# Attention's TensorE stream tied to program order, x written a unit later, no pairs of v beside the last rows' scores

## The chip, the cores and the metric

The kernel runs on one NeuronCore of a Trainium2 chip. The metric is device time in microseconds, the median of three runs: 1057.58 us before the change (1056.65 to 1059.66). Engines are named as in the profile: PE is TensorE, DVE is VectorE, ACT is ScalarE, POOL is GpSimd, SP is SyncE.

## The reference, cut to what matters

Attention over 4 batches, 8 heads, 576 positions and 64 dimensions, with a learned bias on the distance of two positions; then a mixture of eight experts that picks one for each token; then a dense block. All in 32-bit floats.

```python
scores = scale * q @ k^T + bias          # [4, 8, 576, 576]
attn   = exp(scores - max);  attn /= sum(attn) + 1e-9
x      = attn @ v                        # -> [2304, 512]
logits = x @ w_gate + modality_bias[modality_id];  e = argmax(logits)
x      = gate * (relu(x @ w1[e]) @ w2[e])
h      = x @ w_in;  out = (h * sigmoid(1.702 * h)) @ w_out
```

## The kernel before

Three stages follow each other: attention (to about 360 us of the span), routing and experts, the dense block. Only attention's code is touched.

Attention works in 16 groups g = 4 * hp + b (a pair of heads hp of one batch b). A group has five units: c = 0 to 3 are 128 rows of queries of both heads, c = 4 is the last 64 rows of both heads together. The list `order` holds all 80 units. Groups 0 to 3 are interleaved at first; from unit 20 on (group 4) a group's five units stand in a row, so that unit 5g + c is row block c of group g. The loop over i (L732 ff.) works at unit u = i + 2 on several things:

- `qkT(u)`, the scores: for c < 4 twelve matmuls into two buffers of PSUM (sc, one for each head, each half the array's rows, written in turn so that the two heads' matmuls run beside each other), for c = 4 six matmuls into one. DVE adds the bias and takes the maximum (L570, p, one instruction for each head), ACT takes the exponential (L574) and sums each row into rs.
- `tps(i)`, two units later: the exponentials p are transposed on PE through PSUM (tp_0, tp_1: four transposes each, tp_r: one) and copied into pt. DVE copies tp_0, ACT copies tp_1 and tp_r (L597, L599, L602). For c = 4 there are tp_0 and tp_r alone, and of each ACT copies one head (L608, L612) and DVE then the other (L609, L613); the DVE copy waits for the ACT copy.
- the product with v, in pieces from the list `todo`: `rest` (L639, one matmul that opens the sum in PSUM, pv) and four `pair`s (L645, two and two in two units). A group has two such products: part 0 for c = 0 and 1 (256 columns), part 1 for c = 2, 3 and 4 (320 columns). After the last pair ACT copies pv into xt (L649).
- `xs()`, called x below: xt is turned and multiplied with the gate's weights on PE (L666, L669, six matmul passes for part 1 and four for part 0), and DVE makes the logits and the output rows from it (Lp L685, xo L701 and L707), which go to X in DRAM.
- two steps of the next group's q and k: ACT rounds them (qh L524), DVE takes the rest (ql L529).
- now and then a step that prepares a block of the dense weights (cva, wh, wl: L168 to L195), and in the last groups sums of the logits (Lacc L692).

PSUM has three pools here: psb with two buffers for the scores, pst with three for tp and x, psv with a single one for pv. A buffer is written again only when its reader is done: pv's first matmul of a product waits for the copy xt of the product before, and an x that follows tp_0, tp_1 and tp_r takes the buffer of tp_0 and so waits for DVE's copy of it.

The order on each engine is not the code's order. A scheduler goes through the code, weighs costs and places each instruction when it thinks its inputs ready; `tc.keep_in_program_order` or `issue_after` bind single ones. The engines then take their instructions strictly in the order that came out. Once built, tp, p, sc and so on carry the unit's number, pv, xt and x the group's and the part's: sc51_0 are the scores of head 0 in unit 51 (c = 1 of group 10), x9_0 is x of part 0 of group 9.

Of the kernel before, what the change touches and what calls it, by code (L numbers as in the profile page):

```python
# [9 lines left out]
F32 = mybir.dt.float32  # L10
# [105 lines left out]
def body(ctx, tc, qk, vv, few, mid, ew1, ew2, ww, cst, alog, out, dbg=None):  # L116
    nc = tc.nc
    pe, act, dve, pool, sp = nc.tensor, nc.scalar, nc.vector, nc.gpsimd, nc.sync
# [10 lines left out]
    psv = acx.enter_context(tc.tile_pool(name="psv", bufs=1, space=PSUM))  # L129

    pso = None

    def big(name):
        return psb.tile([128, 2, 512], F32, tag="big", name=name)
# [143 lines left out]
    def routing_prepare(rp):  # L278
        def tl(name, *shape, dt=F32):
            V[name] = rp.tile([128, *shape], dt, name="r_" + name)  # L280
            return V[name]
        V["tl"] = tl
        pool.tensor_copy(tl("tri", 128, dt=F16), cc(C_TRI, 128))
        pool.memset(tl("ones", 128, dt=F16), 1.0)
        pool.tensor_copy(tl("iota", 128, dt=F16), cc(C_IOTA, 128))
        pool.memset(tl("zz", E * NTILE), 0.0)
        pool.memset(tl("cum", 1 + E * NTILE), 0.0)
        pool.memset(sn, 1)
        tl("mx", NTILE), tl("m2", NTILE), tl("dl", NTILE, E), tl("sc", NTILE, E), tl("A", E, NTILE, dt=F16)
# [162 lines left out]
    def attention():  # L452
        cx = ExitStack()
        kp = cx.enter_context(tc.tile_pool(name="akeep", bufs=1))
        p2 = cx.enter_context(tc.tile_pool(name="a2", bufs=2))
# [63 lines left out]
        def prep_steps(g):  # L519

            def hi(h):
                if h == 0:
                    hi_[g] = own(g, "qh", [128, 2, 640], F32R)
                act.copy(hi_[g][:, h], raw[g][:, h])  # L524

            def lo(h):
                if h == 0:
                    lo_[g] = own(g, "ql", [128, 2, 640], F32R)
                dve.tensor_tensor(lo_[g][:, h], raw[g][:, h], hi_[g].bitcast(F32)[:, h], op=ALU.subtract)  # L529
            return [lambda: hi(0), lambda: hi(1), lambda: lo(0), lambda: lo(1)]  # L530

        un = {}
        grp = {}
        todo = []


        order = [(0, 0), (1, 0), (0, 1), (1, 1), (2, 0), (2, 1), (3, 0), (3, 1)]
# [41 lines left out]
        def tps(i):  # L579
            g, c = order[i]  # L580
            G = grp[g]
            p = un.pop(i)["p"]
            half = 0 if c < 2 else 1
            if c in (0, 2):
                w_ = 256 if c == 0 else 320
                G["pt", half] = p2.tile([128, 9, 320], F32, tag="pt", name=f"pt{g}_{half}")[:, :, :w_]
            pt = G["pt", half]
            if c < 4:
                col = 128 * (c - 2 * half)
                for h in range(2):  # L590
                    ps = pst.tile([128, 512], F32, tag="t", name=f"tp{i}_{h}")
                    for cc in range(4):
                        c0 = 640 * h + 128 * cc
                        pe.transpose(ps[:, 128 * cc:128 * cc + 128], p[:, c0:c0 + 128], ident)  # L594
                    dst, src = pt[:, 4 * h:4 * h + 4, col:col + 128], ps.rearrange("p (c r) -> p c r", c=4)
                    if h == 0:
                        dve.tensor_copy(dst, src)  # L597
                    else:
                        act.copy(dst, src)  # L599
                ps = pst.tile([128, 512], F32, tag="t", name=f"tp{i}_r")  # L600
                pe.transpose(ps[:, :128], p[:, 512:640], ident)
                act.copy(pt[:, 8, col:col + 128], ps[:, :128])  # L602
            else:
                ps = pst.tile([128, 512], F32, tag="t", name=f"tp{i}_0")
                for cc in range(4):
                    pe.transpose(ps[:, 128 * cc:128 * cc + 128], p[:, 128 * cc:128 * cc + 128], ident)
                s_ = ps.rearrange("p (c h r) -> p h c r", c=4, h=2)
                act.copy(pt[:, 0:4, 256:320], s_[:, 0])  # L608
                dve.tensor_copy(pt[:, 4:8, 256:320], s_[:, 1])  # L609
                ps = pst.tile([128, 512], F32, tag="t", name=f"tp{i}_r")  # L610
                pe.transpose(ps[:64, :128], p[:, 512:S], ident)
                act.copy(pt[0:64, 8, 256:320], ps[0:64, 0:64])  # L612
                dve.tensor_copy(pt[64:128, 8, 256:320], ps[0:64, 64:128])  # L613
            if c == 1:
                todo.extend(pv_pieces(g, 0))
            if c == 3 and g == 15:
                *pv, G["xs"] = pv_pieces(g, 2)
                todo.extend(pv)
            if c == 4:
                if g == 15:  # L620
                    *pv, xs = pv_pieces(g, 3)
                    todo.extend(pv + [G["xs"], xs])
                else:
                    todo.extend(pv_pieces(g, 1))

        def pv_pieces(g, part):


            G = grp[g]
            hp, b = divmod(g, B)  # L630
            half = min(part, 1)
# [10 lines left out]
            def pair(cc):  # L642
                ps = G["ps", part]
                for h in range(2):
                    pe.matmul(ps[64 * h:64 * h + 64, :W], lhsT=vm[g][:, 256 * h + 64 * cc:256 * h + 64 * cc + 64],  # L645
                              rhs=G["pt", half][:, 4 * h + cc, cols], start=False, stop=cc == 3)
                if cc == 3:
                    xt = G["xt", part] = p2.tile([128, 320], F32, tag="xt", name=f"xt{g}_{part}")[:, :W]
                    act.copy(xt, ps[:, :W])  # L649
                    ri = G["ri", part] = p2.tile([128, 3, 2], F32, tag=f"ri{half}", name=f"ri{g}_{part}")  # L650
                    if main:
                        dve.tensor_scalar_add(ri[:, 0:2], G["rs", 2 * half], 1e-9)
                    if tail:
                        pool.memset(ri[64:128, 2, :], 1.0)
                        for h in range(2):
                            dve.tensor_scalar_add(ri[0:64, 2, h:h + 1], G["rs", 4][64 * h:64 * h + 64], 1e-9)
                    used = ri[:, 0 if main else 2:3 if tail else 2]
                    dve.reciprocal(used, used)
# [63 lines left out]
            def two(a):  # L722
                for cc in (a, a + 1):
                    pair(cc)
            return [(rest, lambda: two(0)), (None, lambda: two(2)), (xs, None)]

        load_qkv(1)
        nT = 0
# [3 lines left out]
        vcx = ExitStack()  # L732
        NU = 80
        pend = []
        for i in range(-2, NU + 6):
            u = i + 2
            if u < NU:
                while nT < need.get(u, 36):
                    bias_step(nT)
                    if nT in (1, 4):  # L740
                        for f in prep_steps(0 if nT == 1 else 1):
                            f()
                    if nT % 8 == 0 and nT:
                        load_bias(0, nT // 8 - 1)
                    nT += 1
                    if nT == 36:
                        bias_evac()
                        load_bias(0, 4)
                        bcx.close()
                        modality()  # L750
                if u == 25:
                    ecx.close()
                    wpool["w0"] = ctx.enter_context(tc.tile_pool(name="w0", bufs=1, side="right"))
                    routing_prepare(rcx.enter_context(tc.tile_pool(name="rp", bufs=1, side="right")))
                    wpool["cv"] = vcx.enter_context(tc.tile_pool(name="cv", bufs=1, side="right"))
                    early = conv_list(list(range(4)))
                if u in starts:
                    load_qkv(starts[u])
                    pend = prep_steps(starts[u])


            if u >= NU and i < NU:
                tps(i)
            steps = todo[:1]
            if len(todo) > 1 and (not todo[0][1] or len(todo) > 4 and todo[1][1]):
                steps = todo[:2]
            del todo[:len(steps)]
            if 0 <= i and u < NU:
                tps(i)
            for whole, _ in steps:  # L770
                if whole:
                    whole()
            if u < NU:
                qkT(u)
            for _, half in steps:
                if half:
                    half()
            for _ in range(3 if u < 8 else 2):
                if pend and (u < 8 or u not in starts):
                    pend.pop(0)()  # L780
            if early and u % 2:
                early.pop(0)()
        assert not todo
        while early:
            early.pop(0)()
        vcx.close()
# [338 lines left out]
```

## Time and profile before

| | |
|---|---|
| median of three runs | 1057.58 us |
| the profiled execution, its own time | 1058.45 us |
| its span | 1056.8 us |
| PE busy over the span | 1012.0 us (96%) |
| DVE, ACT busy over the span | 749.5 us (71%), 629.9 us (60%) |
| attention's steady part, unit 24 to unit 79 | 143.77 to 347.12 us, 203.35 us, eleven cycles |

The profile lists busy time by engine, the waits (who waited for whom), and timelines with each group of instructions in order of time. Matmuls are pipelined: the duration of a row is longer than its distance to the next, so the cost of a block on PE is read from the start of its row to the start of the next block's row. The steady part repeats every five units, from the scores of c = 4 of one group to those of the next; this is called a cycle below.

### The profile page before, as it was taken

The page shows a single profiled execution, that of the slowest core. Times are in us where ns is not written, and L with a number is a line of the kernel's source. Part 1 is how long each engine was busy: PE and PEld are TensorE (multiplying, and loading weights), DVE is VectorE, ACT ScalarE, POOL GpSimd, SP SyncE. Part 2 cuts the span into 40 slices and gives each one's busy share as a digit, 9 for nine tenths or more (in the row PEclk, how much of TensorE's full clock was granted, in tenths as well). Part 3 has the DMA queues.
Part 4 walks back from the last instruction along what each step waited for, and adds up shares of the span by engine and source line. Part 5 has one row for each costly group of instructions (what it writes and reads, how often), then busy time and mean ns, then how long its engine had stood idle before and what let it go on. Part 6 is the DMA issues. An engine that isn't in the chain of part 4 may idle for free. (4 is left out here: it accounts for less than half of the span.)

```text
span 1056.8 us, 17322 instructions
## 1 busy us (share of the span) xinstructions
PE 1012.0 (96%) x6030; PEld 810.5 (77%) x6030; DVE 749.5 (71%) x1476; ACT 629.9 (60%) x1203; POOL 131.1 (12%) x136
## 2 busy tenths in 40 slices
PE   6899999999999679999999999999999999999997
PEld 2447666676676458888888888999998899999996
DVE  7977777787877789999999984734574566464433
ACT  7867667676666469999899973534432333232221
POOL 6400000000000153651111000000000000001212
PEclk9999999999999889999999999999999999999999
DMA  8755412523410151511252352400220112010111
GB/s 285 259 174 171 123 45 85 184 82 93 143 43 18 53 184 38 203 41 51 80 187 83 101 178 94 139 31 21 61 80 1 41 44 77 1 40 31 48 43 60
DMA packets 46939, 98.08 MB, mean 93 GB/s; under 512 B 7424, under 2 KB 16896, under 8 KB 46848
## 3 DMA queue, kind: packets, MB, share of 16 engines
q1 hardware_dynamic: 41904, 80.90, 24.0%
q0 software_dynamic: 4800, 15.73, 4.2%
q8 instruction: 49, 0.80, 0.3%
q14 instruction: 42, 0.34, 0.1%
q10 hardware_dynamic: 144, 0.29, 0.1%
HBM read 146.57 MB, written 25.84 MB: 163 GB/s over the span
## 5 line engine op out<-in xcount | busy, mean ns | idle before, releaser
L828 DVE TENSOR_TENSOR wl<-wraw,wh 128x1024 fp32r<-128x1024 f32 x167 | 198.3, 1241 | 7.1 <-ACT wh L826 4.9
L826 ACT CAST wh<-wraw 128x1024 fp32r<-128x1024 f32 x168 | 171.3, 1064 | 16.6 <-PE p L853 8.3
L1018 ACT ACTIVATE sg<-f 128x384 f32<-128x384 f32 x96 | 47.2, 491 | 178.0 <-PE f L1015 178.0
L1020 DVE TENSOR_TENSOR gg<-f,sg 128x384 f32<-128x384 f32 x96 | 53.4, 556 | 139.8 <-ACT sg L1018 139.7
L574 ACT ACTIVATE p<-p,mx 128x576 f32<-128x576 f32 x144 | 110.8, 771 | 50.1 <-DVE mx L570 48.6
L1015 PE MATMUL f<-yh,wh 128*128 128x384 f32 x384 | 129.9, 338 | 1.0 <-ACTq L967 1.0
L1015 PE MATMUL f<-yh,wl 128*128 128x384 f32 x384 | 129.5, 337 | 0.0
L1015 PE MATMUL f<-yl,wh 128*128 128x384 f32 x384 | 129.5, 337 | 0.0
L570 DVE CUSTOM_DVE_ANT_0 p<-sc,bias 128x576 f32<-128x576 f32 x144 | 104.2, 751 | 17.6 <-PE sc L562 17.0
L1048 PE MATMUL o<-wh,gl 128*128 128x512 f32 x288 | 114.0, 396 | 0.0
L1048 PE MATMUL o<-wh,gh 128*128 128x512 f32 x288 | 113.4, 394 | 0.0
L1048 PE MATMUL o<-wl,gh 128*128 128x512 f32 x288 | 113.4, 394 | 0.0
L1023 ACT CAST gh<-gg 128x384 fp32r<-128x384 f32 x96 | 49.2, 513 | 52.5 <-DVE gg L1020 51.0
L645 PE MATMUL pv<-pt,v 128*64 128x256 f32 (+2 forms) x528 | 78.4, 411 | 0.0
L594 PEld LDWEIGHTS tp<-cs,p 128*128 128x128 f32 x512 | 55.0, 141 | 27.9 <-issue 15.4
L1015 PEld LDWEIGHTS f<-yh,wh 128*128 128x128 f32 x384 | 72.1, 188 | 5.2 <-ACTq L967 1.4
L1024 DVE TENSOR_TENSOR gl<-gg,gh 128x384 fp32r<-128x384 f32 x96 | 53.5, 558 | 30.7 <-ACT gh L1023 30.7
L1015 PEld LDWEIGHTS f<-yl,wh 128*128 128x128 f32 x384 | 72.1, 188 | 4.1
L594 PE MATMUL tp<-cs,p 128*128 128x128 f32 x512 | 71.9, 281 | 0.7 <-ACT p L574 0.4
L1015 PEld LDWEIGHTS f<-yh,wl 128*128 128x128 f32 x384 | 72.1, 188 | 0.0
L853 PE MATMUL p<-wh,xh 128*128 128x512 f32 x168 | 67.6, 406 | 0.0
L853 PE MATMUL p<-wl,xh 128*128 128x512 f32 x168 | 66.3, 395 | 1.2 <-DVE wl L828 1.2
(186 smaller groups left out, 2061.0 us busy)
## 6 DMA issues: line engine op xcount, KB each, us to landing
wraw<-in_moe_w_dram SPq DMA_DIRECT2D x176, 512.0 KB
cvraw<-in_ww_dram SPq DMA_DIRECT2D x32, 512.0 KB
biasD<-bev SPq DMA_DIRECT2D x36, 295.5 KB
raw<-in_qk_dram SPq DMA_DIRECT2D x16, 640.0 KB
Yc<-y POOLq DMA_DIRECT2D x21, 256.0 KB
v<-in_vv_dram SPq DMA_DIRECT2D x16, 320.0 KB
bias<-biasD SPq DMA_DIRECT2D x16, 288.0 KB
yi<-Yc SPq DMA_DIRECT2D x18, 256.0 KB
```

The source lines that it names most:

```text
L570: dve.tensor_tensor_reduce(out=pp.rearrange("p (a j) -> p a j", a=2), in0=ps[:, :, :288], in1=bt[:, h].rearrange("p (a j) -> p a j", a=2), ...
L574: act.activation(pp, pp, AF.Exp, bias=mx[:, h:h + 1], scale=-1.0, accum_out=rs[:, c % 2, h:h + 1] if c < 4 else rs)
L594: pe.transpose(ps[:, 128 * cc:128 * cc + 128], p[:, c0:c0 + 128], ident)
L645: pe.matmul(ps[64 * h:64 * h + 64, :W], lhsT=vm[g][:, 256 * h + 64 * cc:256 * h + 64 * cc + 64], rhs=G["pt", half][:, 4 * h + cc, cols], s ...
L826: act.copy(h, t)
L828: V["split"] = by.tensor_tensor(l, t, h.bitcast(F32), op=ALU.subtract).ins
L853: pe.matmul(out, lhsT=a[x_], rhs=b[y_], start=first and i == 0, stop=last and i == 2)
L1015: pe.matmul(ps, lhsT=w[x_][:, 128 * k_:128 * k_ + 128], rhs=y_[:, k_, :], start=k_ == 0 and n_ == 0, stop=k_ == 3 and n_ == 2)
L1020: dve.tensor_tensor(gg, ps, sg, op=ALU.mult)
L1023: act.copy(gh, gg)
L1024: dve.tensor_tensor(gl, gg, gh.bitcast(F32), op=ALU.subtract)
L1048: pe.matmul(po[t_], lhsT=a_[:, sl_], rhs=b_, start=fc == 0 and n_ == 0, stop=fc == 3 and n_ == 2)
```

## The change

All of PE's instructions from unit 8 to the end of attention are tied in the order in which the code writes them, each to the one before. x is no longer an entry of `todo` but goes to the list `outs`, due two units after the last pairs, and is written right after that unit's transposes. In a unit with c = 4 nothing is taken from `todo` unless three pieces wait. pt gets a third buffer. The end of the last group is written in another order.

```diff
--- before.py
+++ after.py
@@ -129,6 +129,20 @@
     psv = acx.enter_context(tc.tile_pool(name="psv", bufs=1, space=PSUM))
 
     pso = None
+
+    def traced():
+        return nc.cur_bb.bb.instructions
+
+    def as_written(start, engines):
+
+        for engine in engines:
+            last = None
+            for i in traced()[start:]:
+                if i.engine == engine:
+                    if last is not None:
+                        tc.add_manual_dep(i, last.name, mybir.DependencyInfo(
+                            mybir.DependencyClass.NoSync, mybir.DependencyReason.DATA), reason="as_written")
+                    last = i
 
     def big(name):
         return psb.tile([128, 2, 512], F32, tag="big", name=name)
@@ -531,7 +545,7 @@
 
         un = {}
         grp = {}
-        todo = []
+        todo, outs, now = [], [], [0]
 
 
         order = [(0, 0), (1, 0), (0, 1), (1, 1), (2, 0), (2, 1), (3, 0), (3, 1)]
@@ -583,7 +597,7 @@
             half = 0 if c < 2 else 1
             if c in (0, 2):
                 w_ = 256 if c == 0 else 320
-                G["pt", half] = p2.tile([128, 9, 320], F32, tag="pt", name=f"pt{g}_{half}")[:, :, :w_]
+                G["pt", half] = p2.tile([128, 9, 320], F32, tag="pt", bufs=3, name=f"pt{g}_{half}")[:, :, :w_]
             pt = G["pt", half]
             if c < 4:
                 col = 128 * (c - 2 * half)
@@ -614,14 +628,9 @@
             if c == 1:
                 todo.extend(pv_pieces(g, 0))
             if c == 3 and g == 15:
-                *pv, G["xs"] = pv_pieces(g, 2)
-                todo.extend(pv)
+                todo.extend(pv_pieces(g, 2))
             if c == 4:
-                if g == 15:
-                    *pv, xs = pv_pieces(g, 3)
-                    todo.extend(pv + [G["xs"], xs])
-                else:
-                    todo.extend(pv_pieces(g, 1))
+                todo.extend(pv_pieces(g, 3 if g == 15 else 1))
 
         def pv_pieces(g, part):
 
@@ -722,7 +731,10 @@
             def two(a):
                 for cc in (a, a + 1):
                     pair(cc)
-            return [(rest, lambda: two(0)), (None, lambda: two(2)), (xs, None)]
+            def last():
+                two(2)
+                outs.append((now[0] + 2, xs))
+            return [(rest, lambda: two(0)), (None, last)]
 
         load_qkv(1)
         nT = 0
@@ -732,8 +744,10 @@
         vcx = ExitStack()
         NU = 80
         pend = []
-        for i in range(-2, NU + 6):
-            u = i + 2
+        for i in range(-2, NU + 5):
+            u = now[0] = i + 2
+            if u == 8:
+                start = len(traced())
             if u < NU:
                 while nT < need.get(u, 36):
                     bias_step(nT)
@@ -761,26 +775,28 @@
 
             if u >= NU and i < NU:
                 tps(i)
-            steps = todo[:1]
-            if len(todo) > 1 and (not todo[0][1] or len(todo) > 4 and todo[1][1]):
-                steps = todo[:2]
+
+            steps = todo[:0 if u < NU and order[u][1] == 4 and len(todo) < 3 else 1 if len(todo) < 5 else 2]
             del todo[:len(steps)]
             if 0 <= i and u < NU:
                 tps(i)
-            for whole, _ in steps:
-                if whole:
-                    whole()
+            while outs and (outs[0][0] <= u or u >= NU):
+                outs.pop(0)[1]()
+            if steps and steps[0][0]:
+                steps[0][0]()
             if u < NU:
                 qkT(u)
-            for _, half in steps:
-                if half:
-                    half()
+            for n, (whole, half) in enumerate(steps):
+                if n and whole:
+                    whole()
+                half()
             for _ in range(3 if u < 8 else 2):
                 if pend and (u < 8 or u not in starts):
                     pend.pop(0)()
             if early and u % 2:
                 early.pop(0)()
-        assert not todo
+        assert not todo and not outs
+        as_written(start, [pe.engine])
         while early:
             early.pop(0)()
         vcx.close()
```

Only PE is tied. The scheduler places DVE's and ACT's instructions anew around it. Three places follow, from group 9 and unit 50 on.

PE from x of group 9's part 0 to unit 52. Before (lines of the kernel before):

```order
L666 MATMUL x9_0_3151<-rhw_109,xt9_0_3135 128x144 x2
L562 MATMUL sc51_0_3160<-qh10_2948,ql10_2994 128x288
L562 MATMUL sc51_1_3161<-qh10_2948,ql10_2994 128x288
L594 MATMUL tp50_0_3184<-cs_72,p50_3110 128x128 x4
L594 MATMUL tp50_1_3190<-cs_72,p50_3110 128x128 x4
L601 MATMUL tp50_r_3196<-cs_72,p50_3110 128x128
L639 MATMUL pv9_1_3199<-pt9_1_3045,v9_2627 128x320
L562 MATMUL sc52_0_3204<-qh10_2948 128x288
```

With the change (L576 is L562, L608 is L594, L654 is L645, L648 is L639):

```order
L576 MATMUL sc51_1_3145<-qh10_2941,ql10_2987 128x288
L654 MATMUL pv9_0_3104<-pt9_0_2944,v9_2610 64x256 x4
L608 MATMUL tp50_0_3177<-cs_72,p50_3106 128x128 x4
L608 MATMUL tp50_1_3183<-cs_72,p50_3106 128x128 x4
L615 MATMUL tp50_r_3189<-cs_72,p50_3106 128x128
L648 MATMUL pv9_1_3192<-pt9_1_3045,v9_2610 128x320
L576 MATMUL sc52_0_3197<-qh10_2941 128x288
```

x9_0 is gone from between the scores of unit 51 (it now follows the transposes of unit 51, in unit 53); in its place the last two pairs of pv9_0 stand behind these scores, and pv9_1 opens after the next nine transposes. Before, those pairs stood one unit earlier. The scores of the two heads alternate now throughout.

ACT between unit 50's and unit 51's exponentials (p50, p51). Before:

```order
L574 ACTIVATE p50_3110,rs10_0_3112<-p50_3110,mx50_3111 128x576 x2
L649 COPY xt9_0_3135<-pv9_0_3072 128x256
L608 COPY pt9_1_3045<-tp49_0_3140 128x4x64
L612 COPY pt9_1_3045<-tp49_r_3147 64x64
L599 COPY pt10_0_3183<-tp50_1_3190 128x4x128
L574 ACTIVATE p51_3158,rs10_0_3112<-p51_3158,mx51_3159 128x576 x2
L602 COPY pt10_0_3183<-tp50_r_3196 128x128
```

With the change:

```order
L588 ACTIVATE p50_3106,rs10_0_3108<-p50_3106,mx50_3107 128x576 x2
L622 COPY pt9_1_3045<-tp49_0_3131 128x4x64
L626 COPY pt9_1_3045<-tp49_r_3138 64x64
L588 ACTIVATE p51_3142,rs10_0_3108<-p51_3142,mx51_3143 128x576 x2
L658 COPY xt9_0_3166<-pv9_0_3104 128x256
L613 COPY pt10_0_3176<-tp50_1_3183 128x4x128
L616 COPY pt10_0_3176<-tp50_r_3189 128x128
```

and ten units later, with the change:

```order
L588 ACTIVATE p60_3591,rs12_0_3593<-p60_3591,mx60_3592 128x576 x2
L622 COPY pt11_1_3526<-tp59_0_3616 128x4x64
L626 COPY pt11_1_3526<-tp59_r_3623 64x64
L658 COPY xt11_0_3651<-pv11_0_3589 128x256
L588 ACTIVATE p61_3627,rs12_0_3593<-p61_3627,mx61_3628 128x576 x2
```

The copy xt9_0, which frees the one pv buffer, stood behind the exponentials of unit 50; it now stands behind those of unit 51. Of the eleven cycles five are like this one (xt6_0, xt7_0, xt9_0, xt10_0, xt14_0); in six, as in the last rows, the copy stands ahead of that unit's exponentials (xt4_0, xt5_0, xt8_0, xt11_0, xt12_0, xt13_0). The same holds in the early part once, for xt2_1, behind the exponentials of unit 21.

PE around the scores of c = 4 in unit 49. Before:

```order
L566 MATMUL sc49_0_3077<-ql9_2760,qh9_2712 128x288
L666 MATMUL x8_1_3061<-rhw_109,xt8_1_3037 128x144 x2
L669 MATMUL x8_1_3061<-rhw_109,xt8_1_3037 64x144
L639 MATMUL pv9_0_3072<-pt9_0_2951,v9_2627 128x256
L566 MATMUL sc49_0_3077<-qh9_2712,ql9_2760 128x288
L645 MATMUL pv9_0_3072<-pt9_0_2951,v9_2627 64x256 x4
L594 MATMUL tp48_0_3095<-cs_72,p48_3013 128x128 x4
L594 MATMUL tp48_1_3101<-cs_72,p48_3013 128x128 x4
L601 MATMUL tp48_r_3107<-cs_72,p48_3013 128x128
L562 MATMUL sc50_0_3113<-qh10_2948 128x288
```

With the change:

```order
L580 MATMUL sc49_0_3064<-qh9_2705,ql9_2753 128x288
L608 MATMUL tp48_0_3078<-cs_72,p48_3013 128x128 x4
L608 MATMUL tp48_1_3084<-cs_72,p48_3013 128x128 x4
L615 MATMUL tp48_r_3090<-cs_72,p48_3013 128x128
L675 MATMUL x8_1_3093<-rhw_109,xt8_1_3037 128x144 x2
L678 MATMUL x8_1_3093<-rhw_109,xt8_1_3037 64x144
L648 MATMUL pv9_0_3104<-pt9_0_2944,v9_2610 128x256
L576 MATMUL sc50_0_3109<-qh10_2941 128x288
```

x8_1 no longer cuts the scores of unit 49 but stands right behind the nine transposes of unit 48. The same place, nine transposes and then x, is found for part 0 in front of each unit with c = 3. After attention the order on PE, DVE and ACT is the same in both kernels.

## Rows read from the trace of the kernel before

**Rows 1.** Stretches: length, then busy time of PE, PEld, DVE, ACT, POOL; PEclk; DMA.

```profile
87.47:143.77 56.30, 55.36 (x436) 38.88 (x435) 39.88 (x119) 36.99 (x98) 1.39 (x9) 1.00 0.37 113
143.77:347.12 203.35, 198.83 (x1555) 140.20 (x1553) 156.11 (x457) 137.40 (x359) 0.95 (x10) 1.00 0.29 89
```

**Rows 2.** Waits of PE, 143.77 to 347.12: engine, line, releaser, total us, times, longest.

```profile
PE x L666 <- ACT xt L649: 4.2, 10, 0.8
```

**Rows 3.** Timeline of PE, one cycle: start us, us, instruction, [idle before].

```profile
236.34 0.76 PE L666 MATMUL x<-rhw,xt 128*128 128x144 f32 x4
...
237.42 0.70 PE L639 MATMUL pv<-pt,v 128*128 128x256 f32 x2
...
240.33 0.40 PE L562 MATMUL sc<-qh 64*128 64x288 f32 x2
...
241.31 1.08 PE L645 MATMUL pv<-pt,v 128*64 128x256 f32 x8
242.32 0.66 PE L606 MATMUL tp<-cs,p 128*128 128x128 f32 x4
...
243.02 0.58 PE L562 MATMUL sc<-qh 64*128 64x288 f32 x2
...
244.50 0.76 PE L666 MATMUL x<-rhw,xt 128*128 128x144 f32 x4 [0.37 <-ACT xt L649]
245.19 0.40 PE L562 MATMUL sc<-qh,ql 64*128 64x288 f32 x2
245.52 1.09 PE L594 MATMUL tp<-cs,p 128*128 128x128 f32 x8
...
246.56 0.70 PE L639 MATMUL pv<-pt,v 128*128 128x320 f32 x2
247.19 0.59 PE L562 MATMUL sc<-qh 64*128 64x288 f32 x2
...
251.71 1.30 PE L645 MATMUL pv<-pt,v 128*64 128x320 f32 x8
252.94 1.10 PE L594 MATMUL tp<-cs,p 128*128 128x128 f32 x8
```

**Rows 4.** Timeline of DVE, the same cycle.

```profile
239.05 0.83 DVE L529 TENSOR_TENSOR ql<-raw,qh 128x640 fp32r<-128x640 f32 x1
...
241.23 0.30 DVE L656 TENSOR_SCALAR ri<-rs 64x1 f32<-64x1 f32 x2
...
241.74 0.72 DVE L570 CUSTOM_DVE_ANT_0 p<-sc,bias 128x576 f32<-128x576 f32 x1
...
244.75 0.42 DVE L609 COPY pt<-tp 128x256 f32<-128x256 f32 x1 [1.60 <-ACT pt L608]
...
245.46 0.19 DVE L685 TENSOR_TENSOR Lp<-x,ri 128x32 f32<-128x32 f32 x1
...
251.82 0.76 DVE L570 CUSTOM_DVE_ANT_0 p<-sc,bias 128x576 f32<-128x576 f32 x1 [0.79 <-PE sc L562]
...
253.64 0.69 DVE L597 COPY pt<-tp 128x512 f32<-128x512 f32 x1 [0.38 <-PE tp L594]
...
255.85 0.37 DVE L685 TENSOR_TENSOR Lp<-x,ri 128x32 f32<-128x32 f32 x2 [1.34 <-PE x L669]
...
256.80 0.74 DVE L570 CUSTOM_DVE_ANT_0 p<-sc,bias 128x576 f32<-128x576 f32 x1
```

**Rows 5.** Timeline of ACT, the same cycle.

```profile
242.57 0.78 ACT L574 ACTIVATE p<-p,mx 128x576 f32<-128x576 f32 x1 [1.49 <-DVE mx L570]
...
244.10 0.35 ACT L649 COPY xt<-pv 128x256 f32<-128x256 f32 x1
244.35 0.37 ACT L608 COPY pt<-tp 128x256 f32<-128x256 f32 x1
```

**Rows 6.** Two early stretches, columns as in rows 1.

```profile
30.00:34.00 4.00, 2.42 (x24) 1.79 (x20) 2.95 (x9) 3.32 (x9) 0.47 (x1) 1.00 0.97 372
34.00:45.00 11.00, 9.38 (x81) 4.52 (x73) 10.60 (x27) 9.57 (x23) 6.19 (x8) 0.86 0.78 239
```

## The prediction

> **What bounds the kernel now.** First the page's shares by engine (the table above): PE is busy 96% of the span, so only its own stream counts, and only attention's part of it is touched. Next the busy time by stretch [rows 1]: in the eleven steady cycles PE is busy 198.83 of 203.35 us, DVE 156.11, ACT 137.40. PE bounds the stage and idles 4.5 us in it. Then PE's waits there [rows 2]: 4.2 us in ten waits, all of them x waiting for ACT's copy xt. That is the stop the change is aimed at. Last, the timelines of one cycle, unit 49 to 53 [rows 3 to 5], where the reader is to see three things. (a) The scores of unit 51 run from 243.02, x cuts in at 244.50 after 0.37 us of idle, the last two matmuls come at 245.19 and the transposes at 245.52: the block takes 1.81 us without x, where the uncut one of unit 50 takes 0.98 (240.33 to 241.31). (b) x came late because ACT copied xt (244.10) only behind both exponentials, 2.36 us after DVE began with the scores (241.74). (c) DVE sat idle 1.60 us until ACT had copied the other head of c = 4, and only then, at 245.46 and later, got to the next scores. DVE and ACT are far from full, but each takes its list strictly in order, so a late copy holds up everything behind it. A mean cycle is 203.35 / 11 = 18.49 us.
>
> **PE's work alone, with the change.** Nothing is added or taken away on PE; blocks are moved. Block lengths, start to start [rows 3]: twelve scores 0.98; pairs of 256 columns 1.01 (241.31 to 242.32); pairs of 320 columns 1.23 (251.71 to 252.94); five transposes of c = 4 0.70 (242.32 to 243.02); nine transposes 1.04 (245.52 to 246.56); the opening matmul of pv with 320 columns 0.63 (246.56 to 247.19), with 256 by that some 0.50 (an estimate); x of four 0.69 (244.50 to 245.19), of six 1.08 (236.34 to 237.42). For the six scores of c = 4, uncut, I take 0.98 too (an estimate: six steps like the six pairs). The sum: 5 x 0.98 + 2 x 1.01 + 2 x 1.23 + 0.70 + 4 x 1.04 + 0.50 + 0.63 + 0.69 + 1.08 = 17.14. So the uncut order is worth up to 18.49 - 17.14 = 1.35 us a cycle, of which 0.4 is recorded idle and the rest is cut score blocks and heads that did not alternate. The question is what PE now waits for.
>
> **The cycle walked through**, t = 0 at the scores of c = 4. They end at 0.98, and the nine transposes follow at once.
> - x of part 1 now stands behind these transposes and needs the buffer of the first four. DVE is with the scores from 0.98 + 0.11 (251.71 on PE to 251.82 on DVE [rows 3, 4]) for 0.76, to 1.85. The first copy could start 0.70 after the transposes (252.94 to 253.64), which is 1.68, so it starts at 1.85 and takes 0.69, to 2.54. A wait ends 0.05 after its releaser (244.10 + 0.35 on ACT, 244.50 on PE [rows 3, 5]). x starts at 2.59, not at 2.02: **a wait of 0.57**.
> - x 1.08, opening 0.50, scores of c = 0: end at 5.15. Pairs, transposes of c = 4: 6.86.
> - DVE meanwhile: two ql of 0.83 behind the copy, to 4.20; Lp and xo 0.95 (255.85 to 256.80), to 5.15; three ri 0.51 (241.23 to 241.74), to 5.66. There it begins with the scores of c = 0, 0.4 late. Both heads take about 1.4, so the second buffer is free at 7.1 and the scores of c = 1 lose **0.2**: they end at 8.04. Pairs to 9.05, nine transposes to 10.09: there PE wants to open pv for part 1, in the one pv buffer.
> - ACT's exponentials of c = 0 are done 2.36 after DVE's start, at 8.02. Without xt in between, the copies of c = 4 follow; DVE's begin 0.40 after ACT's (244.35 to 244.75) and take 0.71 (244.75 to 245.46): 9.13. Only now does DVE begin with the scores of c = 1; ACT has both exponentials at 11.49 and then copies xt in 0.35. Where xt stands behind these exponentials, as the order has it in five cycles of eleven, pv opens at 11.89: **a wait of 1.80**. In the other six ACT copies xt at about 9.5 and there is none.
> - Opening 0.63, scores 0.98, pairs 1.23, then nine transposes and x of part 0, which again waits for DVE's copy: 0.70 + 0.69 + 0.05 = 1.44 behind the transposes' start in place of 1.04, **a wait of 0.40**. Then x 0.69, scores 0.98, pairs 1.23, transposes 1.04.
>
> The long kind of cycle comes to 20.11 us, the short kind to 18.31. Some short ones also carry splits of a weight block or sums of logits on DVE ahead of the scores of c = 0, each less than a ql of 0.83; I take 18.5 for a short one (18.3 to 18.9). Eleven cycles: 5 x 20.1 + 6 x 18.5 = 211.5, which is **+8.2 us**.
>
> **The early part** (units 8 to 24, 56.30 us [rows 1]). Added: five x behind nine transposes, 0.40 to 0.57 each, 2.4; pv's buffer at unit 22 behind the exponentials of unit 21, 1.5; two smaller ones of that kind at units 9 and 11, together up to 1.0. Removed: 0.9 of recorded idle (the stretch has 56.30 - 55.36) and five cut score blocks, each 0.46 beyond its idle (1.81 - 0.98 - 0.37), 2.3. Net +1.7; between 0 and +3. **The end** of the last group: pv's opening and one x now stand right behind the copy they need, against one more part that is done early: 0 to +1, I take 0.5. The third pt buffer costs nothing by itself: no engine does more for it. POOL, SP and the DMAs do the same work; the stores of x start up to two units (some 7 us) later inside attention, and the last ones stand where they stood. Routing, experts and the dense block keep their order on every engine.
>
> **The sum**: 8.2 + 1.7 + 0.5 = +10.4, on the profiled execution 1058.45 + 10.4 = 1068.9. That execution is 0.87 above the median of the runs, so on the median 1057.58 + 10.4 = 1068.0 us.
>
> **A rule against the trace.** In the trace of before no opening matmul of pv waits for ACT [rows 2]: a single pv buffer costs nothing there, since a unit lay between the two products. The Trainium skill, Perfetto Trace Analysis, section Matmuls, says that independent groups of matmuls should rotate through different PSUM banks so that ACT or DVE empties one while the next runs. By the row alone the pv wait would be 0 and a long cycle would be a short one; by the rule it is the whole way of the copy, and the sum above takes that side, with the length from rows 3 to 5.
>
> **The rivals.**
> 1. *Faster: the waits do not form.* The cycle falls to PE's own 17.14: 11 x 1.35 = 14.9 less, and the early part gives its 3.2 back: 1039.5. This decides itself at one point: xt must be copied within 10.09 - 5.66 = 4.4 us of DVE's start with c = 0, and x's buffer within 1.04 of the transposes. Against it: rows 4 and 5 show 3.7 us for the first half of that way alone (241.74 to 245.46), and 1.38 for the buffer. Chance 0.05.
> 2. *No change: only the long wait is missing.* If the exponentials of c = 1 come earlier than I think, all eleven cycles are short: 11 x 18.4 = 202.4, -1 us, with early part and end at +1: 1057.6. For it: x's waits (0.4 to 0.6) about balance the stop removed. Against it: the lists of ACT and DVE fix the chain. Chance 0.13.
> 3. *Slower still: lateness adds up.* If DVE's delay at c = 0 is a ql longer in every cycle (0.83), as where weight splits stand there, both kinds grow by up to 0.7: 11 x 0.7 = 7.7 more, 1075.7. Chance 0.08.
> 4. *The clock.* The granted clock is 1.00 all through these cycles [rows 1]. Early, with PE busy 2.42 of 4 us, it stayed at 1.00 (2.4 GHz); in 34 to 45 us it averaged 0.86, so some 3 of 11 us ran at the lower level (1.2 GHz), a loss of 1.5 us [rows 6]. If each of the six long waits brought such a fall, that would be 9 us more: 1077. The Trainium skill, TensorE: Matmul & The Clock Gate, section "A second HAM failure mode: psum-queue depth-cycling", describes short PE idling between matmul groups that makes the clock swing. Ten stops of up to 0.8 us [rows 2] left it at 1.00 here, and PE would still be busy over nine tenths of the stage. Chance 0.04.
>
> That the change does not do what it says is ruled out by the order of the built program.
>
> **How the numbers follow.** Forecast 0.70, rivals 0.05, 0.13, 0.08, 0.04. A measurement of this kernel can tell about 0.3%, 3.2 us, from no change: 1054.4 to 1060.8 is the same. Faster takes rival 1 and a little of rival 2: 0.06. Same takes the rest of rival 2: 0.12. Slower 0.82. The forecast's own bounds: short cycles 18.3 to 18.9 (-1.2, +2.4), early part -1.7 to +1.3, end -0.5 to +0.5: 1064.6 to 1072.2. To leave out no more than 0.2 the range goes down to 1060, where most of rival 2 and rival 1 are left out, and up to 1074, toward rival 3.
>
> **What would show it.** In the waits of PE: x waiting for ACT's xt gone, in its place x waiting for DVE's pt (some 16 waits, 0.4 to 0.6 us each) and pv's opening waiting for ACT's xt (six of some 1.5 to 1.8 us). Score blocks of 0.98 nearly everywhere. Cycles of two lengths, about 20 and 18.5, the long ones in the five groups named. PEclk 1.00 in the stage. If all cycles have one length, the long wait was mis-sized; if x has no waits, DVE reaches the copies sooner than I read.

## The result: 1% slower

The changed kernel takes 1068.96 us (median of four, 1066.87 to 1069.43), the kernel before beside it 1058.19 (1056.65 to 1059.66). The ratio is 1.0098, with a 95% interval of 1.0078 to 1.0119. The profiled execution is the fastest of the four, 1066.87 us, with a span of 1065.2 us against 1056.8 before: 8.4 us more.

Lines are renumbered: the scores are L576 (c = 4: L580), transposes L608 and L615, pv's opening L648, pairs L654, x L675 and L678, the copy xt L658, the exponential L588. First the stretches of the changed kernel, columns as in rows 1: the eleven cycles, then a long one and a short one of them.

```profile
144.61:354.36 209.75, 194.38 (x1554) 135.78 (x1553) 158.25 (x457) 136.13 (x359) 1.72 (x10) 1.00 0.29 86
181.01:200.85 19.84, 17.66 (x144) 12.29 (x143) 13.51 (x39) 12.03 (x33) 0.09 (x1) 1.00 0.51 155
297.80:316.02 18.22, 17.50 (x145) 12.37 (x142) 14.05 (x43) 12.13 (x33) 0.09 (x1) 1.00 0.12 36
```

Against [rows 1] the stage is 209.75 - 203.35 = 6.40 us longer. PE is busy 4.45 us less, with blocks no longer cut (in run 6, where they are cut again, it is busy 198.43 us in the eleven cycles), and idle 15.4 us where it was 4.5. The rest of the 8.4 us: the first scores of c = 4 in the stage start 0.84 later, and the end of the last group takes 1.16 longer (15.79 us from those of unit 79 to rk, a matmul of the routing, against 14.63). After attention nothing is added.

PE's waits in the same stretch, columns as in rows 2:

```profile
PE pv L648 <- ACT xt L658: 7.4, 5, 1.6
PE x L675 <- DVE pt L611: 6.9, 20, 0.5
PE tp L608 <- ACT pt L613: 0.7, 2, 0.3
PE sc L576 <- DVE mx L584: 0.3, 1, 0.3
```

x waiting for xt [rows 2] is gone. In its place stand twenty waits of x for DVE's copy, of 0.24 to 0.48 us each, and five of pv's opening for xt. The timeline of PE in one long cycle of the changed kernel:

```profile
240.39 1.04 PE L608 MATMUL tp<-cs,p 128*128 128x128 f32 x8
...
242.01 0.76 PE L675 MATMUL x<-rhw,xt 128*128 128x144 f32 x4 [0.47 <-DVE pt L611]
...
246.41 0.40 PE L576 MATMUL sc<-qh 64*128 64x288 f32 x2
...
247.40 1.08 PE L654 MATMUL pv<-pt,v 128*64 128x256 f32 x8
248.41 1.09 PE L608 MATMUL tp<-cs,p 128*128 128x128 f32 x8
...
251.08 0.81 PE L648 MATMUL pv<-pt,v 128*128 128x320 f32 x2 [1.46 <-ACT xt L658]
251.81 0.40 PE L576 MATMUL sc<-qh 64*128 64x288 f32 x2
...
254.03 1.09 PE L608 MATMUL tp<-cs,p 128*128 128x128 f32 x8
...
255.47 0.76 PE L675 MATMUL x<-rhw,xt 128*128 128x144 f32 x4 [0.24 <-DVE pt L611]
```

ACT's timeline ahead of that long wait:

```profile
247.20 0.35 ACT L622 COPY pt<-tp 128x256 f32<-128x256 f32 x1
247.45 0.20 ACT L626 COPY pt<-tp_r 64x64 f32<-64x64 f32 x1
249.15 0.78 ACT L588 ACTIVATE p<-p,mx 128x576 f32<-128x576 f32 x1 [1.49 <-DVE mx L584]
...
249.92 0.76 ACT L588 ACTIVATE p<-p,mx 128x576 f32<-128x576 f32 x1
...
250.68 0.35 ACT L658 COPY xt<-pv 128x256 f32<-128x256 f32 x1
```

And DVE's, from the scores of the unit before (c = 0) on:

```profile
244.81 0.76 DVE L584 CUSTOM_DVE_ANT_0 p<-sc,bias 128x576 f32<-128x576 f32 x1 [0.16 <-PE sc L576]
...
247.58 0.42 DVE L623 COPY pt<-tp 128x256 f32<-128x256 f32 x1 [1.33 <-ACT pt L622]
...
248.29 0.76 DVE L584 CUSTOM_DVE_ANT_0 p<-sc,bias 128x576 f32<-128x576 f32 x1
```

The last pairs are over at 248.41, and ACT does nothing from 247.65 to 249.15. It could copy xt there, but the exponentials of the scores just made stand ahead of that copy, and they wait for DVE. DVE was idle for 1.33 us too, because its copy L623 stands ahead of the scores and waits for ACT's L622. So PE stops for 1.46 us (1.62 by the blocks' starts) for a copy of 0.35.

### The profile page after: what moved, and what is told of

Read it like the earlier page. It is cut to its first block, busy times and chain, and to the rows that moved or that the text cites. A ratio compares the mean times of both kernels' runs of the same rounds, so it can differ in the third digit from the quotient of the medians.

```text
span 1065.2 us, 17247 instructions
## 1 busy us (share of the span) xinstructions
PE 1005.0 (94%) x6030; PEld 804.3 (76%) x6030; DVE 752.3 (71%) x1476; ACT 627.8 (59%) x1203; POOL 131.6 (12%) x136
## 5 line engine op out<-in xcount | busy, mean ns | idle before, releaser
L588 ACT ACTIVATE p<-p,mx 128x576 f32<-128x576 f32 x144 | 110.9, 771 | 95.0 <-DVE mx L584 94.5
L654 PE MATMUL pv<-pt,v 128*64 128x256 f32 (+2 forms) x528 | 77.8, 411 | 0.0
L608 PEld LDWEIGHTS tp<-cs,p 128*128 128x128 f32 x512 | 55.8, 141 | 27.9 <-issue 16.1
L608 PE MATMUL tp<-cs,p 128*128 128x128 f32 x512 | 71.8, 280 | 1.9 <-ACT pt L613 1.7
L869 PE MATMUL p<-wh,hh 128*128 128x512 f32 x168 | 66.9, 398 | 0.0
```

What stands on the lines that cost most here:

```text
L588: act.activation(pp, pp, AF.Exp, bias=mx[:, h:h + 1], scale=-1.0, accum_out=rs[:, c % 2, h:h + 1] if c < 4 else rs)
L869: pe.matmul(out, lhsT=a[x_], rhs=b[y_], start=first and i == 0, stop=last and i == 2)
```

## The experiments

All ratios are to the kernel before, run on the same chip. "Cycles" are the eleven of the steady part of each profiled execution.

| | ties | x later | no pairs at c = 4 | us, median | ratio (95%) | eleven cycles, us |
|---|---|---|---|---|---|---|
| before | no | no | no | 1058.2 to 1058.9 | 1 | 203.35 |
| changed | yes | yes | yes | 1068.96 | 1.0098 (1.0078 to 1.0119) | 209.75 |
| 1: xt ahead | yes | yes | yes | 1057.73 | 0.9995 (0.9981 to 1.0008) | 201.02 |
| 2: xt behind | yes | yes | yes | 1081.65 | 1.0225 (1.0203 to 1.0246) | 224.49 |
| 3: x behind the scores | yes | yes | yes | 1056.54 | 0.9975 (0.9965 to 0.9984) | 201.88 |
| 4: pairs back | yes | yes | no | 1081.81 | 1.0217 (1.0192 to 1.0241) | 220.55 |
| 5: ties alone | yes | no | no | 1077.18 | 1.0172 (1.0155 to 1.0189) | 218.11 |
| 6: no ties | no | yes | yes | 1057.48 | 0.9991 (0.9981 to 1.0000) | 200.63 |
| 7: 1 and 3 | yes | yes | yes | 1041.24 | 0.9835 (0.9819 to 0.9852) | 188.48 |
| 8: 7 without ties | no | yes | yes | 1041.66 | 0.9851 (0.9834 to 0.9869) | 188.58 |
| 9: 4 with 7 | yes | yes | no | 1054.27 | 0.9964 (0.9951 to 0.9976) | 198.93 |

### 1. The copy of xt ahead of the exponentials

In units with c = 1, qkT leaves DVE's and ACT's work on the scores to a function, which is called behind the pairs.

```diff
-            for h, ps in enumerate(pss):
+            def post():
+              for h, ps in enumerate(pss):
...
+            if u_late(i):
+                G["post"] = post
+            else:
+                post()
...
+            if u_late(u):
+                with tc.issue_after(copies[-1].ins):
+                    grp[order[u][0]].pop("post")()
```

> The changed kernel with ScalarE's queue alone reordered: in the units with the first rows' second half (from group 2's second part on) the scores' maxima and exponentials are queued behind the pairs and the copy of xt. TensorE's order is untouched. Theory (the opening of the second product waits because the copy of xt stands behind the new scores' exponentials in ScalarE's queue): the five waits of 1.6 us and the one at unit 22 go, the five long cycles of 19.8 us become 18.3; five times 1.5 and 1.5 are 9 us, so about 1060 us (1057 to 1063), and no wait of over 1 us of the opening for xt stays. Rival (the wait belongs to the tied order, the pairs simply a unit later): the waits stay and the time is 1066 to 1070. Second rival (TensorE is gained but the exponentials, now later, delay the transposes two blocks on): 1063 to 1067, with waits of the transposes for the exponentials in the place of the others.

It took 1057.73 us, 11.2 less than the changed kernel (between the medians). The cycles are 8.73 us shorter: the five long ones come to 18.1, the six others stay within 0.03. From the first scores of c = 4 to those of unit 24 it takes 49.82 us, 1.32 less, which answers to the wait at unit 22. The two profiled spans differ by 7.6 us only: this execution came to the first scores of c = 4 some 2.8 us later, with a granted clock of 0.83 from 30 to 50 us of the span where the changed kernel's had 0.91. The timeline of ACT at the same place of the cycle:

```profile
246.57 0.37 ACT L668 COPY xt<-pv 128x256 f32<-128x256 f32 x1 [0.88 <-PE pv L664]
247.19 0.78 ACT L594 ACTIVATE p<-p,mx 128x576 f32<-128x576 f32 x1 [0.24 <-DVE mx L590]
```

PE's timeline there:

```profile
246.46 1.09 PE L618 MATMUL tp<-cs,p 128*128 128x128 f32 x8
247.38 0.27 PE L625 MATMUL tp_r<-cs,p 128*128 128x128 f32 x1
247.49 0.70 PE L658 MATMUL pv<-pt,v 128*128 128x320 f32 x2
```

All of PE's waits of this run in the stage:

```profile
PE x L685 <- DVE pt L621: 6.9, 20, 0.5
PE tp L618 <- ACT pt L623: 0.7, 2, 0.3
PE sc L581 <- DVE mx L590: 0.3, 1, 0.3
```

ACT copies as soon as the last pair is done, and pv opens right behind the transposes, with no row for its wait in the stage. The other two lines are those of the changed kernel unchanged: nothing was shifted onto the transposes. PE's order is the same, and DVE's place is too: it begins with these scores 1.87 us after PE does, 1.88 in the changed kernel. So in this order of PE the long wait is set by ACT's queue. Both rivals fall.

### 2. The copy of xt behind the exponentials everywhere

```diff
-                    act.copy(xt, ps[:, :W])
+                    late = 20 < now[0] < NU and order[now[0]][1] == 1
+                    with tc.issue_after(exps[0].ins) if late else ExitStack():
+                        act.copy(xt, ps[:, :W])
```

> The changed kernel with the copy of xt of part 0 queued behind the new scores' exponentials in every cycle instead of five of eleven. Nothing else moves. Theory: six more cycles turn long, each by the 1.5 us that separates the long cycles (19.8) from the short ones (18.3); 9 us, so about 1078 us (1075 to 1081), and all eleven cycles at 19.8. Rival (long cycles are long for another reason that goes with these five groups, their lengths or data): the time stays at 1066 to 1070 and the other six cycles stay at 18.3.

It took 1081.65 us. The direction is the theory's, and eleven openings now wait instead of five (17.7 us in all); the rival falls. But the size, +12.7, lies above the range. Four of the six cycles grow by 1.84 to 1.94, not 1.5, and two by 3.55 and 3.62. In those two the pause is longer (1.83 and 2.05 us), and what follows runs slowly. The PE timeline of one of them:

```profile
177.20 1.11 PE L650 MATMUL pv<-pt,v 128*128 128x320 f32 x2 [1.83 <-ACT xt L662]
178.24 0.61 PE L578 MATMUL sc<-qh 64*128 64x288 f32 x2
```

Three stretches of this run, columns as in rows 1: up to the opening behind that pause, behind it, and behind the other one:

```profile
174.00:177.20 3.20, 1.37 (x14) 0.97 (x10) 3.10 (x10) 2.37 (x7) 0.00 (x0) 1.00 0.54 164
177.20:181.70 4.50, 4.50 (x23) 2.45 (x23) 1.58 (x5) 1.35 (x4) 0.00 (x0) 0.62 0.02 4
341.00:345.00 4.00, 4.00 (x24) 2.16 (x23) 1.45 (x4) 1.63 (x4) 0.00 (x0) 0.57 0.01 4
```

The score block behind the pause takes 1.74 us (178.24 to 179.98) instead of 0.98. The clock was 1.00 up to the pause and 0.62 and 0.57 behind it, mostly its lower level (1.2 GHz). By the lengths of the blocks, 1.04 + 1.74 + 1.70 us against 0.74 + 0.98 + 1.23, the first fall costs 1.5 us, and the second, worked out likewise, 1.6.

### 3. x behind the scores

```diff
-            while outs and (outs[0][0] <= u or u >= NU):
-                outs.pop(0)[1]()
             if steps and steps[0][0]:
                 steps[0][0]()
             if u < NU:
                 qkT(u)
+            while outs and (outs[0][0] <= u or u >= NU):
+                outs.pop(0)[1]()
```

> The changed kernel with the unit's x written behind the unit's scores instead of between the last transposes and the scores, so its operands have a block of scores more to come. Theory by the sum: the 7.9 us of x waiting for the transposes' copies go; the opening of the second product stands 1.1 us (the x of part 1) further from the pairs, so that the five waits of 1.6 shrink to 0.5 or so, another 5 us; together 10 to 14 us, 1055 to 1059 us. Rival (the waits of x are harmless, TensorE only meets the same copies a block later): 1065 to 1069, with waits of 0.5 us in front of the scores or the pairs in their place.

1056.54 us: the total is as expected, its parts are not. PE's waits in the stage:

```profile
PE pv L648 <- ACT xt L658: 11.1, 9, 1.4
PE sc L576 <- DVE mx L584: 0.9, 4, 0.3
```

x's waits for DVE's copy are gone; their rival falls. But pv's opening now waits some 1.2 us in nine cycles, not 0.5 in five: with x written elsewhere the scheduler's order for ACT, which is not tied, came out with xt behind the exponentials in nine of the eleven. What x's place cost is more than the recorded idle. From the start of the nine transposes to the start of the next block it took 1.62 and 1.44 us in the changed kernel, where that block is x, and takes 0.98 and 1.13 here, where no x stands behind them.

### 4. Pairs back beside the last rows' scores

```diff
-            steps = todo[:0 if u < NU and order[u][1] == 4 and len(todo) < 3 else 1 if len(todo) < 5 else 2]
+            steps = todo[:1 if len(todo) < 5 else 2]
```

> The changed kernel with one of its three parts undone: pairs of v are again taken beside the last rows' scores. The opening of part 0 then no longer comes one unit after the pairs of part 1. Theory (the long wait comes from dropping these pairs, which moves the opening next to the copy that it needs): the waits of 1.6 us go or come to under 0.4, about 1058 to 1062 us; what stays are the waits of x, 8 us in all. Rival (the ties alone make the long wait): 1066 to 1070.

This theory fell: 1081.81 us, 12.9 slower than the changed kernel. The openings do wait less, as it said (6.8 us in twelve waits of 0.57 in the mean, up to 1.0), but x waits more (9.5 us in 22) and a new wait of transposes comes in (3.9 in ten). The unit left without pairs is now c = 1, with full scores, and not c = 4 with half of them. The PE timeline there:

```profile
255.85 0.40 PE L576 MATMUL sc<-qh 64*128 64x288 f32 x2
...
256.84 0.66 PE L608 MATMUL tp<-cs,p 128*128 128x128 f32 x4
257.76 0.66 PE L608 MATMUL tp<-cs,p 128*128 128x128 f32 x4 [0.27 <-DVE pt L623]
...
259.10 0.76 PE L675 MATMUL x<-rhw,xt 128*128 128x144 f32 x4 [0.57 <-ACT pt L613]
```

ACT's timeline at the same place:

```profile
255.87 0.76 ACT L588 ACTIVATE p<-p,mx 128x576 f32<-128x576 f32 x1
256.54 0.19 ACT L588 ACTIVATION_READ_ACCUMULATOR p<-p,mx 128x1 f32 x1
256.63 0.35 ACT L658 COPY xt<-pv 128x256 f32<-128x256 f32 x1
256.89 0.37 ACT L622 COPY pt<-tp 128x256 f32<-128x256 f32 x1
```

PE is at the next transposes a block of pairs (1.0 us) early, while ACT has yet to empty the ones before. From the transposes' start to x it is 2.26 us, where nine transposes take 1.04. Run 9 tests that reading. In one cycle the clock fell as in run 2 (a mean of 0.92 over the 22 us), with no pause above 1.05 us in it.

### 5. The ties alone

The kernel before with `as_written` called for PE from unit 8 on, and nothing else of the change.

> The kernel before with the ties alone: TensorE's instructions of attention in the program's order, x and the pairs where they were. x then comes with its pairs of the unit before only one unit old, ahead of the scores, with no block moved in between. Theory (the tied order makes each wait that the scheduler had filled with other blocks): x waits for xt or for its copies in every cycle, and the sum is 6 to 12 us slower than the kernel before, 1064 to 1070 us. Rival (the ties are harmless and the moved x and pairs make the loss): 1056 to 1060.

1077.18 us, 18.8 slower than before, beyond the theory's range but on its side; the rival falls. Waits of x for xt [rows 2] go from 4.2 us in ten to 21.4 in 21:

```profile
PE x L679 <- ACT xt L662: 21.4, 21, 1.9
```

The scheduler had let x cut into a block of scores when its operand came; tied, x stops PE in its written place, in one cycle for 1.40 us and 0.52. Here too the clock fell, in two cycles (0.92 over 22 us each), behind a pause of 1.47 us in one and of 1.93 in the other.

### 6. The change without the ties

```diff
-        as_written(start, [pe.engine])
```

> The changed kernel without the ties: x a unit later and no pairs beside the last rows' scores, with TensorE's order left to the scheduler. Theory: the scheduler puts a block of scores in front of an opening or an x whose operand is late, so most of the 1.6 us waits go; 1055 to 1062 us. Rival (the loss comes from dropping the pairs and the later x, whoever orders TensorE): 1066 to 1070.

1057.48 us, the kernel before again: the whole loss of 11.5 us is with the ties, given this order of the code. But this run moves more than PE's order, since the scheduler places ACT's instructions anew: xt now stands ahead of the exponentials in seven cycles, among them four of the five long ones of the changed kernel. So it does not tell PE's order from ACT's; run 8 does. Without the ties pv's opening waits 1.2 us in three waits and x 0.3 in one.

### 7. Edits 1 and 3 together

> The two edits together: the copies of xt ahead of the exponentials, and x behind the scores. Theory: neither the opening nor x waits, the cycles come to 17.1 to 17.8 us, PE's own work in the cycle plus small gaps, so 1040 to 1052 us, faster than both kernels. Rival (VectorE's and ScalarE's work in turn, or the exponentials now late, are the next bound at 18.3 us a cycle): 1055 to 1061, with waits for the exponentials or the maxima in the place of the others.

1041.24 us, 1.65% faster than before and 2.6% than the changed kernel. The stage of this run, columns as in rows 1:

```profile
140.70:329.18 188.48, 187.39 (x1555) 135.51 (x1553) 155.92 (x457) 138.36 (x358) 1.34 (x10) 1.00 0.32 96
```

All of PE's waits in it:

```profile
PE sc L581 <- DVE mx L590: 0.9, 4, 0.3
```

A mean cycle is 188.48 / 11 = 17.13 us; seven of the eleven take 16.88 to 16.92, and two with waits for DVE's maxima take 17.81 and 18.21. DVE and ACT do what they did in [rows 1] (155.92 and 138.36 us), so they were not the next bound at 18.3. PE issues as many matmuls as before and is busy 187.39 us for them instead of 198.83.

### 8. The same without the ties

> The two edits together (copies of xt ahead of the exponentials, x behind the scores), with the ties taken out, so that the scheduler orders TensorE again. Theory (once no operand is late in the written order, the order itself is worth keeping, since the scheduler puts single blocks between others by its own estimate): 1043 to 1050 us, a few us slower than the same kernel with ties at 1041.2. Rival (the loss of the change comes with the ties and without them everything is better): 1036 to 1041.

1041.66 us and cycles of 188.58: no difference, between the theory and its rival. With xt ahead of the exponentials in all eleven cycles of either run, it does not matter here who orders PE.

### 9. Pairs back, with both edits

Edit of run 4 with those of run 7, the scores' work held back in every unit that ends a product.

> Pairs back beside the last rows' scores, which leaves the unit of the first rows' second half without pairs, but with the copies of xt ahead of the exponentials in every unit that ends a product, and x behind the scores. Theory (the 1081.8 us with the pairs back come from a unit with full scores and no pairs, in which TensorE is at the transposes a block of pairs, 1.0 us, too early for ScalarE and VectorE): cycles stay over 18 us and the time is 1053 to 1066. Rival (they come from the queue of ScalarE and from x's place alone, as in the changed kernel): cycles of 16.9 to 17.4 as with the two edits, 1040 to 1047.

1054.27 us. Cycles are 17.85 to 18.85, mostly 17.87, 0.99 more than the 16.88 of run 7; the range of the time held, and "over 18" was a little high. PE's only wait in the stage:

```profile
PE tp L618 <- DVE pt L633: 7.6, 11, 1.1
```

Its place in the PE timeline of one cycle:

```profile
240.59 0.66 PE L618 MATMUL tp<-cs,p 128*128 128x128 f32 x4
241.85 0.66 PE L618 MATMUL tp<-cs,p 128*128 128x128 f32 x4 [0.61 <-DVE pt L633]
```

One stop in each cycle, in the unit with full scores and no pairs. So with ACT's order and x's place mended, dropping the pairs at c = 4 is worth 1.0 us a cycle under the ties: it leaves the unit with half the scores as the one without pairs. The rest of run 4's loss went with the order of ACT and the place of x.

## Why the prediction was right

The forecast was 1068.0 (1060 to 1074), and 1068.96 came out. By its steps:

- **The cycle.** Long cycles were put at 20.11; they are 19.81 to 19.97, and in the five groups named. Short ones were taken at 18.5; they are 18.18 to 18.83, mean 18.41. Eleven: +6.4 instead of +8.2.
- **x behind the transposes.** Part 1: 0.57 forecast, 0.47 recorded; from the transposes' start to x 1.62 us against 1.61 worked out. Part 0: 1.44 as worked out. The waits are twenty in the stage, not some 16, and half of them are shorter than forecast, 0.24 us recorded.
- **The long wait.** 1.80 forecast, 1.62 by the blocks' starts. Its steps were read right: from DVE's start with the scores of c = 0 to the copies on ACT 2.39 us (244.81 to 247.20; forecast 2.36), to DVE's next scores 1.09 (1.11), to xt 2.39 (2.36). The chain began earlier, since DVE was not the 0.4 us late at c = 0 that the walk has. Run 1 shows the cause: with only the copy's place in ACT's queue changed, the wait is gone.
- **Terms that were off.** The scores of c = 1 lose 0.2 in the walk, and in most cycles lose nothing (0.99). The opening with 256 columns takes 0.63, not 0.50, and the scores of c = 4 0.88, not 0.98; the two estimates cancel.
- **Early part and end.** +0.84 and +1.16 instead of +1.7 and +0.5. The early part is within its bounds of 0 to +3, the end is beyond its 0 to +1: PE waits 1.9 us there, 1.4 of it for xt, where the kernel before has no wait ahead of rk. Before the stage pv's opening waits for xt three times, 2.1 us, with 1.1 the longest.
- **The sum.** On the two profiled executions it is 8.4, not 10.4; between the medians it is 10.8. The executions of the changed kernel that were not profiled have spans 2.0 to 2.6 us longer than the profiled one, and where they lose that is open. Their granted clock is 0.986 or 0.987 against 0.988, by which one to two of these us could be the clock's (an estimate from the means; no trace of them was kept). So the range held for the right reason, and the closeness to 1 us is luck: the parts came 2 us lower than forecast, and the unprofiled executions put as much on top.
- **Rival 1** (1039.5) did not happen. Its price was near: with the waits gone, in run 7, the mean cycle is 17.13 (forecast 17.14) and the time 1041.24. That the cycles agree so closely is partly chance, since x stands elsewhere there and PE's own cycle, without a wait, is 16.88; the longer cycles make up the rest.
- **Rival 4.** The clock stayed at 1.00 in the changed kernel behind five pauses of 1.46, so this rival did not happen. It fell in run 2 behind 1.83 and 2.05, and the forecast had 1.80 for the pause; but the length of a pause does not settle it (last section), so how near the forecast was to this rival is open. The Trainium skill, TensorE: Matmul & The Clock Gate, section "A second HAM failure mode: psum-queue depth-cycling", speaks of brief idling between matmul groups that makes the clock swing. The five pauses of the changed kernel do not show such a swing; runs 2, 4 and 5 do, in one or two cycles of eleven.
- **The rule on PSUM banks.** With one pv buffer the opening did wait, 7.4 us in the stage. That is the side taken from the Trainium skill, Perfetto Trace Analysis, section Matmuls, by which independent groups of matmuls should rotate through different banks. But run 1 takes the wait away with the one buffer, by the order of ACT alone. No run gave pv a second buffer, so what that would do is not shown; nor was the third pt buffer tried alone.

## What to carry to other kernels

Tying PE to the program's order cost nothing here where each operand was ready in time (runs 7 and 8), and 18.8 us where x's was not (run 5). So before tying an engine look at the in-order queues of the engines that empty its buffers, and put the short copy that frees a buffer ahead of long work that itself waits for something else. A busy share of 98% is no floor: the same matmuls were busy 198.83 us before, 194.38 in the changed kernel with their blocks uncut, and 187.39 in run 7, where the waits were gone too. When a unit must go without filler work, choose the one whose other work is least.

## What was not expected of the hardware

In runs 2, 4 and 5 the granted clock fell from 1.00 to its lower level (1.2 GHz) inside the stage, though PE had paused for no more than 2.05 us at a time. In run 2 it had a mean of 0.62 over 4.5 us and 0.57 over 4 us, though PE was busy all that time, and it was back at 1.00 in the stretch after. Each fall there cost some 1.5 us on top of the pause. In run 5 the two cycles with a pause of 1.93 us took 21.58 us with a fall and 20.10 without, so the profiled executions of runs 2, 4 and 5 hold one or two such losses.

The length of the last pause does not tell when it falls. Rows of PE's timeline and stretches of run 5, the latter with columns as in rows 1: a pause of 1.93 us and the stretch behind it, then another of the same length with a stretch 1.7 us behind its end:

```profile
177.26 0.76 PE L679 MATMUL x<-rhw,xt 128*128 128x144 f32 x4 [1.93 <-ACT xt L662]
177.26:182.00 4.74, 4.74 (x41) 3.75 (x43) 3.96 (x13) 2.74 (x8) 0.00 (x0) 1.00 0.45 140
335.13 0.76 PE L679 MATMUL x<-rhw,xt 128*128 128x144 f32 x4 [1.93 <-ACT xt L662]
336.80:339.90 3.10, 3.10 (x13) 2.31 (x11) 2.63 (x8) 1.76 (x5) 0.00 (x0) 0.50 0.17 48
```

The same of run 4, where the fall follows the longest pause of its cycle and a shorter one behind it:

```profile
337.87 0.66 PE L608 MATMUL tp<-cs,p 128*128 128x128 f32 x4 [1.05 <-DVE pt L623]
339.20:342.40 3.20, 3.19 (x12) 2.33 (x14) 1.77 (x8) 0.88 (x3) 0.00 (x0) 0.50 0.14 39
```

In run 2 a pause of 1.70 us left the clock at 1.00, as five of 1.46 did in the changed kernel, while in run 5 it fell in one cycle behind a pause of 1.47. No run varied the pause alone, so what decides is open.
